# One root for the first two chunks, and a new order of all queues, in a gated recurrence with a convolution-gated output

## The chip, the cores and the metric

The kernel runs on one core of a Trainium2 chip. The metric is the device time of one execution in microseconds, given as the median of the runs. The engines are TensorE (PE), VectorE (DVE), ScalarE (ACT), GpSimd (POOL) and SyncE (SP), which issues nearly all DMAs.

## The reference

The inputs have 4 sequences of 6336 steps and 256 channels. With a = sigmoid(a_param), the first half is a gated linear recurrence:

```python
log_a = 8 * sigmoid(r_gate) * log(clip(a, 1e-6, 1 - 1e-6))
a_t   = exp(log_a)
xg    = sqrt(max(1 - a_t * a_t, 1e-6)) * sigmoid(i_gate) * x
h     = a_t[:, t] * h + xg[:, t]        # for each t; y[:, t] = h
```

The second half takes y: a causal convolution of 5 taps per channel gives a gate, and the result is `(sigmoid(conv(y)) * (y @ w_val)) @ w_out`, in float32.

## The kernel before

The 25344 rows (batch times steps) are cut into 51 windows w of 256 or 512 rows, and these into 28 chunks c (the table CHUNKS): chunks 0 and 1 are one window of 256 each (w0, w1), chunk 2 is one of 512 (w2), chunks 3 to 25 are two windows of 512 each (w3 and w4 to w47 and w48), chunk 26 is one of 512 (w49) and chunk 27 one of 256 (w50). Loads arrive with rows on the partitions; the recurrence needs channels on the partitions and time along the free axis, so PE transposes. Sigmoids are computed as tanh. A channel index has two halves h of 128.

There is no scheduler: the program is the string ORDER, read word by word, and each word emits one step. An engine executes its own steps in the order of the string, so ORDER fixes five queues, and waits follow from the data and from the buffers. A word is a step, its window or chunk, its half, and behind an @ the PSUM banks that it uses. The steps:

- `lr.w`, `li.w`, `lx.w` (L290, SP): load of a window of r_gate, i_gate or x. `st.w` (L519, SP): store of a window of the output. `s_wl.k`: loads of the weights; `s_wcast` (L273 to L276, POOL): their casts.
- `ta.c` (L308, ACT): tanh of r for a chunk. `tr.c.h` (L355, PE): its transposes, for a group of chunks (GROUPS). `ex.c.h` (L376, ACT): exp, which gives a_t for that group. `sq.c.h` (L384, POOL) or `sa.c.h` (L392, ACT): the square of it.
- `rt.b` (L403, ACT): the root of 1 - a_t*a_t for a batch of chunks (the table BATCHES). The root needs another table than exp and tanh, so ACT loads a table before and behind each visit (L535, `ACT_TABLE_LOAD`); several `rt` words with no tanh or exp between them are one visit.
- `tb.c` (L311, ACT): tanh of i. `pp.w` (L318, POOL): plus one. `up.w` (L330, POOL): times x. For w0 only `pp.0` and `up.0` are on POOL; for w1, w2 and w6, `xp.w` (L335, PE) copies x into PSUM by a product with the identity and `uv.w` (L344, DVE) does both.
- `nt.c` (L418, PE): the root, transposed back to rows. `xg.c` (L425, DVE): its product with the gated x. `xt.c` (L434, PE): that, transposed to channels.
- `sc.c.h` (L456, DVE): the recurrence as a scan along time.
- `cv.w` (L468, PE): the convolution as 20 matmuls with diagonal weights. `tg.w` (L475, ACT): its tanh. `vl.w` (L483, PE): y @ w_val. `gv.w` (L488, DVE): their product. `ou.w` (L498, PE): the product with w_out. `cd.w` (L506, DVE) or `ca.w` (L508, ACT): the copy of the result out of PSUM.
- `wm.k` (L362, PE): five matmuls of 512 columns with the identity whose result nobody reads.

An engine that stands at a step whose input is not there waits, and everything behind it on that queue waits too. For example, `rt` of the last chunks comes behind the `tg` words that precede it in ORDER, and `nt`, `xg`, `xt` and `sc` of these chunks behind `rt`. Loads are held back by their rings: r and i have four slots of a window each (`NRI`, `NII`), x has four (`NX`).

Of the kernel before, what the change touches and what calls it, by code (L numbers as in the profile page):

```python
# [44 lines left out]
tb.4 s_wcast xp.6@6,7 sc.3.0 tg.2 li.10 li.9 pp.5 ta.8 vl.1@4,5 lx.10 vl.2@2,3 uv.6 sq.6.1 vl.0@0,1 ta.7 gv.2 lr.17  # L45
cv.3@6,7 lx.8 sq.6.0 gv.0 ou.2.0@2,3 gv.1 tb.5 ou.0.0@0 cd.2.0 ou.1.0@1 up.5 tr.7.0@4,5 tg.3 cd.0.0 st.2 vl.3@2,3
lr.16 cd.1.0 ex.7.0 sq.5.1 st.1 tr.7.1@6,7 gv.3 lr.15 st.0 nt.4@0,1 li.12 ex.7.1 pp.7 cv.4@4,5 xg.4 sq.7.0
ou.3.0@2,3 tg.4 vl.4@6,7 cd.3.0 tb.6 pp.8 xt.4@4,5 gv.4 st.3 sq.7.1 li.11 lr.18 sc.4.1 ou.4.0@6,7 li.13 lx.9 wm.4@0
wm.12@0 up.8 rt.4 sc.4.0 pp.9 up.7 cd.4.0 cv.6@4,5 st.4 vl.6@6,7 lx.12 pp.10 li.14 nt.5@2,3 lx.11 sq.8.0 cv.5@0,1
tg.6 xg.5 tb.7 up.10 gv.6 xt.5@2,3 ou.6.0@6,7 sc.5.0 ta.9 li.16 up.9 vl.5@4,5 tg.5 lr.19 cd.6.0 ta.10 pp.11 wm.8@2  # L50
nt.6@0,1 gv.5 st.6 pp.12 li.15 xg.6 tb.8 ou.5.0@4,5 lr.22 up.11 tr.9.0@6,7 sc.5.1 ca.5.0 xt.6@0,1 ex.9.0 st.5
tr.9.1@4,5 lr.20 sc.6.0 lr.21 cv.7@2,3 ex.9.1 sq.8.1 up.12 cv.8@6,7 sc.6.1 tg.8 vl.7@4,5 pp.14 lx.16 lx.15 tg.7
nt.7@6,7 lx.14 sq.9.1 lx.13 tb.9 gv.7 cv.9@2,3 sq.10.1 xg.7 ou.7.0@4,5 tg.9 vl.9@0,1 cd.7.0 ta.11 sq.9.0 xt.7@2,3
gv.9 st.7 cv.10@4,5 li.20 ta.12 li.18 sc.7.0 pp.16 li.17 vl.8@0,1 sq.10.0 vl.10@6,7 tg.10 lr.26 li.19 gv.8
ou.9.0@4,5 pp.13 gv.10 wm.2@2 ou.8.0@0,1 rt.5 up.14 cd.9.0 ou.10.0@6,7 tr.11.1@2 sc.7.1 st.9 up.16 lr.25 cd.10.0
cv.11@4,5 up.13 cd.8.0 st.10 nt.8@6,7 lr.23 tr.11.0@3 st.8 pp.15 xg.8 tg.11 vl.11@0,1 lr.24 lx.18 ex.11.1 up.15
xt.8@6,7 gv.11 lx.17 ex.11.0 nt.9@4,5 sc.8.0 sq.11.1 tb.10 cv.12@0,1 tr.12.0@3 xg.9 ex.12.0 li.22 pp.17 li.21 sc.8.1
# [36 lines left out]
sc.24.0 tr.27.1@7 ca.40.0 cv.44@0,1 ex.27.1 up.47 st.40 cv.43@2,3 ex.26.1 lx.49 sc.24.1 tg.44 sa.27.1 nt.25@6,7
sq.26.1 tg.43 vl.42@0,1 sq.27.0 tb.26 xg.25 vl.44@2,3 sq.26.0 tb.27 vl.43@4,5 gv.42 pp.50 xt.25@6,7 pp.49 gv.44
# [9 lines left out]
def kernel(  # L105
# [82 lines left out]
    with tc.manual_schedule():  # L188
# [378 lines left out]
```

## Time and profile before

| | us |
|---|---|
| median of 3 runs (290.32 to 290.96) | 290.36 |
| the profiled execution, whole | 290.72 |
| its span, first to last instruction | 288.6 |
| ACT busy in it | 273.7 (95%) |
| PE busy | 250.6 (87%) |
| DVE busy | 247.0 (86%) |
| POOL busy | 241.5 (84%) |
| bytes moved | 104.76 MB, 363 GB/s over the span |

The whole time of the profiled execution is its span and 2.1 us around it. Busy times are read beside each other: idle time of an engine costs something only where another one waits for it. Rows of the timeline give start and duration in us from the span's start, the engine, the line and the step's form, and in brackets the idle time of that engine just before it with what ended it.

### The profile page before, as it was taken

The numbers are of one execution on the slowest core, as the hardware profiler recorded it, in microseconds if no ns is written. First come the engines' busy times: TensorE is split into PE (matmuls) and PEld (weight loads), VectorE is DVE, ScalarE is ACT, GpSimd is POOL, SyncE is SP. The second block draws the span as 40 slices with busy tenths as digits, with TensorE's granted clock in tenths as the row PEclk, the third lists the DMA queues.
The fourth block names the chain that finished last, engine by engine and source line by source line (L and its number), as shares of the span: only waits on it lengthen the run. The fifth ranks groups of instructions, "written<-read, shape, count | busy, mean of one in ns | idle before, by whom it ended". The sixth has DMA issues, their size and how long they took to land.

```text
span 288.6 us, 6363 instructions
## 1 busy us (share of the span) xinstructions
PE 250.6 (87%) x2552; PEld 169.4 (59%) x2552; DVE 247.0 (86%) x214; ACT 273.7 (95%) x197; POOL 241.5 (84%) x161
## 2 busy tenths in 40 slices
PE   2397799879898899889898999889799897999993
PEld 1253557547656677466567585467457664676552
DVE  5002899869999999999998999989999999999891
ACT  4999999999999999999999999999999999999754
POOL 1669469999999999999999999999998999496100
PEclk9999999999999999999999999999999999999998
DMA  7999999999999999999999999999999999885554
GB/s 240 396 392 409 407 374 385 357 385 371 403 407 410 410 395 366 375 346 417 418 408 341 376 413 414 418 395 396 351 352 412 420 386 408 263 292 208 199 221 182
DMA packets 29996, 104.76 MB, mean 363 GB/s; under 512 B 3335, under 2 KB 3854, under 8 KB 29966
## 3 DMA queue, kind: packets, MB, share of 16 engines
q1 hardware_dynamic: 29952, 104.35, 93.9%
q8 instruction: 20, 0.33, 0.5%
q14 instruction: 10, 0.08, 0.1%
q10 hardware_dynamic: 14, 0.01, 0.0%
HBM read 78.39 MB, written 25.95 MB: 362 GB/s over the span
## 4 chain that ended last, share of the span: by engine, by line
POOL 31%; PE 20%; DMA 15%; DVE 12%; ACT 12%; issue 7%; SPq 2%; DVEq 0%; ACTq 0%; POOLq 0%
POOL uring L330 14%; POOL ering L384 11%; DMA xring<-in_x_dram 8%; POOL tbring L318 6%; PE banks L468 6%; DMA iring<-in_i_gate_dram 6%; DVE yring L456 5%; DVE tgring L488 4%; PE banks L483 4%; PE banks L498 3%; PE banks L418 3%; ACT aring L376 3%; ACT tbring L311 3%; ACT ering L403 2%; SPq L290 2%
## 5 line engine op out<-in xcount | busy, mean ns | idle before, releaser
L330 POOL TENSOR_TENSOR uring<-tbring,xring 128x1024 bf16<-128x1024 bf16 (+1 forms) x48 | 100.9, 2116 | 11.1 <-DMA xring<-in_x_dram 10.6
L456 DVE TENSOR_TENSOR_SCAN yring<-aring,yring,banks 128x1024 bf16<-128x1024 f32 (+5 forms) x54 | 105.8, 1987 | 0.2
L384 POOL TENSOR_TENSOR ering<-aring 128x1024 f32<-128x1024 f32 (+2 forms) x54 | 91.7, 1715 | 14.7 <-ACT aring L376 14.6
L468 PE MATMUL banks<-yring,diag 64*64 64x512 bf16 (+7 forms) x1080 | 62.9, 361 | 4.6 <-DVE yring L456 3.6
L488 DVE SCALAR_TENSOR_TENSOR tgring<-tgring,banks 128x1024 bf16<-128x1024 bf16 (+1 forms) x51 | 59.3, 1178 | 5.1 <-PE banks L483 2.4
L498 PE MATMUL banks<-wo,tgring 128*128 128x256 bf16 x396 | 51.1, 274 | 7.5 <-DVE tgring L488 4.9
L376 ACT ACTIVATE aring<-banks,khf 128x2048 f32<-128x2048 bf16 (+3 forms) x38 | 53.9, 1467 | 0.4 <-PE banks L355 0.4
L475 ACT ACTIVATE tgring<-banks 128x1024 bf16<-128x1024 f32 (+1 forms) x51 | 50.5, 1007 | 3.0 <-PE banks L468 2.9
L318 POOL TENSOR_SCALAR tbring<-tbring 128x1024 bf16<-128x1024 bf16 (+1 forms) x48 | 49.0, 1030 | 4.4 <-ACT tbring L311 4.3
L498 PEld LDWEIGHTS <-tgring 128*128 128x128 bf16 x396 | 41.4, 114 | 18.6 <-DVE tgring L488 10.5
L483 PE MATMUL banks<-yring,wv 128*128 128x512 bf16 (+4 forms) x216 | 49.6, 361 | 1.6 <-ACT aring L376 0.8
L308 ACT ACTIVATE taring<-rring 128x2048 bf16<-128x2048 f32 (+2 forms) x28 | 47.6, 1718 | 2.4 <-DMA rring<-in_r_gate_dram 2.4
L311 ACT ACTIVATE tbring<-iring 128x2048 bf16<-128x2048 f32 (+2 forms) x28 | 47.9, 1719 | 0.0
L468 PEld LDWEIGHTS <-diag 64*64 64x64 bf16 x1080 | 29.1, 106 | 28.1 <-issue 11.6
L403 ACT ACTIVATE ering<-ering 128x4096 bf16<-128x4096 f32 (+5 forms) x15 | 44.7, 3016 | 0.1
L506 DVE COPY oring<-banks 128x1024 f32<-128x1024 f32 (+1 forms) x36 | 42.0, 1182 | 1.6 <-PE banks L498 1.1
L355 PE MATMUL banks<-ident_b,taring 128*128 128x128 bf16 x396 | 30.2, 230 | 9.4 <-ACT taring L308 7.2
L425 DVE TENSOR_TENSOR uring<-banks,uring 128x2048 bf16<-128x2048 bf16 (+2 forms) x28 | 30.4, 1093 | 6.7 <-PE banks L418 5.7
L355 PEld LDWEIGHTS <-taring 128*128 128x128 bf16 x396 | 26.1, 103 | 15.1 <-ACT taring L308 9.2
L483 PEld LDWEIGHTS <-wv 128*128 128x128 bf16 x216 | 19.9, 98 | 21.3 <-issue 7.1
L418 PE MATMUL banks<-ident,ering 128*128 128x128 f32 x198 | 29.7, 292 | 1.9 <-DVE yring L456 0.9
L418 PEld LDWEIGHTS banks<-ident,ering 128*128 128x128 f32 x198 | 25.9, 207 | 9.1 <-ACT ering L403 3.5
(45 smaller groups left out, 139.7 us busy)
## 6 DMA issues: line engine op xcount, KB each, us to landing
rring<-in_r_gate_dram SPq DMA_DIRECT2D x48, 512.0 KB, 7.9
iring<-in_i_gate_dram SPq DMA_DIRECT2D x48, 512.0 KB, 8.2
xring<-in_x_dram SPq DMA_DIRECT2D x48, 512.0 KB, 7.9
out_dram<-oring SPq DMA_DIRECT2D x48, 512.0 KB, 5.8
rring<-in_r_gate_dram SPq DMA_DIRECT2D x3, 256.0 KB, 4.4
iring<-in_i_gate_dram SPq DMA_DIRECT2D x3, 256.0 KB, 5.8
xring<-in_x_dram SPq DMA_DIRECT2D x3, 256.0 KB, 8.2
out_dram<-oring SPq DMA_DIRECT2D x3, 256.0 KB, 7.4
```

Of the source, the lines that this page charges most:

```text
L311: nc.scalar.activation(**tangent(c, tbring, NTI, iring, NII))
L318: nc.gpsimd.tensor_scalar(out=t, in0=t, scalar1=1.0, scalar2=1.0, op0=ALU.mult, op1=ALU.add)
L330: nc.gpsimd.tensor_tensor(out=u, in0=t1, in1=xt, op=ALU.mult)
L355: nc.tensor.transpose(out=bank[:, o:o + P], in_=taring[:, place(w, NTR), j, h * P:(h + 1) * P], identity=ident_b[:])
L376: nc.scalar.activation(out=dst, in_=src, func=ACT.Exp, scale=khf[:, h:h + 1], bias=khf[:, h:h + 1])
L384: nc.gpsimd.tensor_tensor(out=e, in0=a, in1=a, op=ALU.mult)
L418: nc.tensor.transpose(out=bank[:, k:k + P], in_=ering[:, e + q:e + wins[w] // 2:nq], identity=ident[:])
L456: nc.vector.tensor_tensor_scan(out=yring[:, h, col:col + o1 - o0], data0=aring[:, h, a_at[c] + o0:a_at[c] + o1], data1=xT[:, o0:o1], initi ...
L468: nc.tensor.matmul(out=gp[oh * 64:oh * 64 + 64, h, a:b], lhsT=diag[half * 64:half * 64 + 64, h, k, :], rhs=yring[half * 64:half * 64 + 64, ...
L483: nc.tensor.matmul(out=val[:, m, a:b], lhsT=wv[:, hk, m * P:(m + 1) * P], rhs=yring[:, hk, col:col + b - a], start=(hk == 0), stop=(hk == ...
L488: nc.vector.scalar_tensor_tensor(out=tgring[:, w % NTG, :, 0:wins[w]], in0=tgring[:, w % NTG, :, 0:wins[w]], scalar=1.0, in1=live.pop(("va ...
L498: nc.tensor.matmul(out=ops[:, j * D:(j + 1) * D], lhsT=gv[:, hk, j:wins[w]:J], rhs=wo[:, hk, :], start=(hk == 0), stop=(hk == H - 1))
```

## The change

Three things change, all in tables; no function does.

- BATCHES: chunks 0 and 1 form one batch, so the first two roots become one instruction, and there are 11 batches in place of 12 (a later `rt.b` has a number lower by one).
- ORDER: all five queues are in a new order, and the PSUM banks behind the @ are new. Among it: SP loads lr.0, lr.1 and li.0 first; the first root visit takes chunk 2, then 0 and 1, then 3 and 4; `xp.1`, `uv.1`, `gv.1` and `cd.1` come earlier; `s_wcast` comes ahead of `sq.5.0`; `cv.45` and `tg.45` come ahead of the last root in place of behind it; `lx.50` is issued ahead of st.44 and st.43.
- Five groups `wm` stand in place of eleven. The copies of windows 5, 23, 34 and 39 move from ACT to DVE, those of 17, 33 and 38 from DVE to ACT.

```diff
-BATCHES = [[0], [1], [2], [3, 4], [5, 6, 7], [8, 9, 10], [11, 12, 13], [14, 15, 16], [17, 18, 19], [20, 21, 22],
-    [23, 24, 25], [26, 27]]
+BATCHES = [[0, 1], [2], [3, 4], [5, 6, 7], [8, 9, 10], [11, 12, 13], [14, 15, 16], [17, 18, 19], [20, 21, 22], [23,
+    24, 25], [26, 27]]
...
-s_ident s_small s_kt s_diag lr.2 lr.0 s_wl.3 lr.1 li.0 lr.3 s_wl.2 ta.2 ta.0 lr.4 tr.0.1@0 ta.1 lr.6 tr.2.0@1 tb.0
-lr.5 tr.1.0@2 tr.0.0@3 tr.2.1@4 ex.2.0 li.1 tr.1.1@5 li.2 ex.1.1 li.3 ex.0.1 sq.1.1 lx.0 ex.1.0 li.4 sq.2.0 ex.0.0
-ex.2.1 sq.1.0 ta.3 sq.2.1 pp.0 sq.0.0 ta.4 sq.0.1 tb.1 lr.10 tr.3.0@4,5 tb.2 lr.9 lr.8 tr.3.1@2,3 lr.7 ex.3.0 lx.2
-s_wl.1 up.0 lx.1 ex.3.1 sq.3.0 lx.4 lx.3 wm.10@6 tb.3 sq.3.1 ta.6 pp.4 wm.5@6 wm.3@6 wm.9@6 wm.6@6 sq.4.1 lr.13 ta.5
-li.5 li.6 sq.4.0 li.7 xp.2@2,3 lr.14 pp.3 rt.0 tr.5.0@4,5 lx.6 uv.2 rt.2 up.4 nt.0@0 rt.1 xg.0 rt.3 xt.0@0,1 xp.1@2
-sc.0.0 up.3 nt.1@3 lx.5 nt.2@0 uv.1 s_wl.0 xg.1 xg.2 xt.1@2,3 lx.7 sc.0.1 lr.12 nt.3@0,1 sc.1.0 lr.11 xt.2@6,7
-sc.1.1 ex.5.0 xg.3 tr.5.1@2,3 li.8 sc.2.0 xt.3@0,1 ex.5.1 sq.5.0 cv.0@4,5 sc.2.1 tg.0 sc.3.1 cv.1@6,7 cv.2@2,3 tg.1
+s_ident s_small s_kt s_diag lr.0 lr.1 li.0 s_wl.2 s_wl.3 lr.2 lr.3 ta.0 lr.4 tb.0 ta.1 lr.5 tr.0.1@0 tr.1.1@1
+tr.1.0@2 ta.2 ex.0.1 ex.1.0 lr.6 li.1 tr.2.0@3 tr.0.0@0 tr.2.1@4 ex.2.0 ex.0.0 ex.2.1 li.2 lx.0 li.4 li.3 sq.1.0
+sq.2.0 sq.0.1 sq.0.0 pp.0 ex.1.1 ta.3 wm.17@5 ta.4 wm.13@5 tb.1 tr.3.1@0,1 tb.2 lr.10 up.0 ex.3.1 lr.9 lr.8 lr.7
+lx.1 tr.3.0@4,5 lx.2 li.5 ex.3.0 sq.4.1 lx.3 lx.4 tb.3 ta.6 li.7 ta.5 xp.1@4 sq.2.1 sq.4.0 lr.11 s_wl.1 xp.2@0,1
+uv.1 sq.3.0 sq.1.1 sq.3.1 s_wl.0 rt.1 rt.0 pp.3 pp.4 rt.2 nt.2@4 lr.14 lx.6 li.6 nt.0@5 uv.2 nt.1@3 lr.12 lr.13 xg.0
+xg.1 li.8 tr.5.0@6,7 lx.5 xt.0@0,1 sc.0.1 up.3 sc.0.0 tr.5.1@2,3 up.4 xt.1@0,1 xg.2 ex.5.0 sc.1.0 sc.1.1 nt.3@4,5
+s_wcast xt.2@0,1 lx.7 cv.1@6,7 ex.5.1 xg.3 sc.2.0 sq.5.0 vl.1@4,5 tg.1 gv.1 cv.0@2,3 tb.4 vl.0@6,7 ou.1.0@0 sq.6.1
+xp.6@4,5 cd.1.0 ta.8 sc.2.1 st.1 xt.3@0,1 li.9 li.10 pp.5 uv.6 lx.8 tg.0 sq.6.0 ta.7 gv.0 cv.2@2,3 nt.4@6,7 up.5
...
-ou.42.0@0,1 rt.11 gv.43 ou.44.0@2,3 up.49 ca.42.0 sc.25.1 ou.43.0@4,5 ca.44.0 st.42 cv.45@0,1 ca.43.0 st.44
-cv.46@2,3 sc.25.0 st.43 lx.50 nt.26@7 tg.46 vl.46@4,5 xg.26 tg.45 cv.47@2,3 gv.46 vl.47@0,1 tg.47 ou.46.0@4,5 gv.47
-up.50 vl.45@2,3 ca.46.0 nt.27@0 ou.47.0@6,7 gv.45 st.46 xt.26@4,5 ca.47.0 xg.27 ou.45.0@2,3 sc.26.0 st.47 cv.48@6,7
+tg.44 lx.49 vl.44@6,7 tb.26 sq.27.0 sq.26.0 sq.26.1 xg.25 cv.45@4,5 vl.43@0,1 gv.44 vl.45@2,3 sa.27.1 tb.27 tg.45
+pp.49 gv.43 xt.25@4,5 gv.45 sc.25.1 sc.25.0 rt.10 ou.44.0@0,1 ou.43.0@6,7 ca.44.0 ou.45.0@2,3 ca.43.0 st.44
+cv.46@0,1 nt.26@6 pp.50 up.49 nt.27@7 ca.45.0 st.43 st.45 vl.46@2,3 up.50 cv.47@4,5 tg.46 xg.26 xg.27 gv.46
+xt.26@0,1 tg.47 vl.47@6,7 cv.48@2,3 gv.47 tg.48 ou.46.0@4,5 sc.26.1 vl.48@6,7 ca.46.0 sc.26.0 ou.47.0@2,3 xt.27@4,5
```

More of the change, by code (lines that the diff above doesn't have):

```diff
@@ L48 @@
[L48 to L57, printed above, removed]
@@ new lines @@
+gv.6 xt.5@2,3 sc.5.0 cv.5@4,5 ta.10 li.15 li.16 ou.6.0@6,7 wm.15@0 nt.6@0,1 tg.5 cd.6.0 ta.9 vl.5@6,7 sc.5.1 st.6
+up.10 pp.12 lr.22 lr.21 lr.20 tr.9.1@4,5 gv.5 tb.8 xg.6 tr.9.0@2,3 ex.9.1 lr.19 ou.5.0@6,7 xt.6@0,1 cd.5.0 ex.9.0
+cv.8@4,5 sc.6.1 st.5 up.12 pp.11 pp.14 pp.13 up.11 cv.7@6,7 tg.8 lx.14 li.18 li.17 lx.13 vl.8@2,3 nt.7@4,5 tg.7
+sc.6.0 vl.7@6,7 tb.9 ta.12 xg.7 cv.10@0,1 lr.25 gv.7 xt.7@4,5 ta.11 gv.8 ou.7.0@6,7 cv.9@2,3 cd.7.0 tg.10 sc.7.0
+st.7 sq.10.1 sq.9.0 sq.10.0 sq.9.1 lx.16 tr.11.1@6 tg.9 ou.8.0@0,1 lx.15 cd.8.0 pp.16 tr.12.1@7 vl.9@2,3 rt.4 gv.9
@@ new lines @@
+st.8 vl.10@0,1 lr.24 lr.26 sc.7.1 ou.9.0@2,3 up.14 up.13 cd.9.0 cv.11@4,5 up.16 pp.15 st.9 gv.10 nt.8@2,3 li.19
+lr.23 ou.10.0@0,1 xg.8 ex.12.1 ex.11.1 tg.11 cd.10.0 xt.8@2,3 tr.11.0@7 st.10 sc.8.0 lx.17 tr.12.0@6 vl.11@0,1 tb.10
+sq.11.1 li.20 li.21 ex.12.0 up.15 gv.11 lx.18 li.22 nt.9@4,5 cv.12@0,1 ex.11.0 ou.11.0@6,7 sc.8.1 ta.14 xg.9 pp.18
+pp.17 cv.14@2,3 tg.12 cd.11.0 xt.9@4,5 sq.11.0 up.17 sq.12.0 st.11 ta.13 cv.13@0,1 sc.9.0 lx.20 lr.30 lr.29 tg.14
+tr.13.0@6,7 tg.13 lx.21 nt.10@2,3 sc.9.1 ex.13.0 vl.13@0,1 up.18 gv.13 tb.11 tr.13.1@4,5 vl.12@6,7 lx.22 xg.10
@@ new lines @@
+pp.23 sq.14.0 pp.24 up.24 sc.11.0 li.28 ex.15.1 lr.34 lr.33 lr.32 gv.18 cv.20@6,7 tb.14 up.23 sq.15.1 sc.12.0
+tr.15.0@4,5 tg.20 ex.15.0 ou.18.0@2,3 cv.19@6,7 cd.18.0 sc.12.1 st.18 vl.19@2,3 tg.19 sq.15.0 sq.16.0 lx.26 lr.31
+li.29 lx.25 vl.20@4,5 tb.15 nt.13@6,7 cv.21@0,1 gv.20 ta.18 ou.20.0@4,5 tg.21 sq.16.1 gv.19 xg.13 vl.21@2,3
+ou.19.0@6,7 cd.20.0 xt.13@0,1 st.20 gv.21 pp.25 pp.26 lx.27 cd.19.0 up.26 up.25 cv.22@4,5 vl.22@2,3 ou.21.0@6,7
+st.19 li.30 sc.13.0 cd.21.0 wm.19@0 pp.27 rt.6 sc.13.1 st.21 nt.14@6,7 lx.28 tg.22 up.27 xg.14 cv.23@0,1 ta.17 gv.22
@@ new lines @@
+xt.14@6,7 pp.28 tg.23 tr.17.1@4,5 sc.14.0 lr.37 lr.38 lr.36 lr.35 vl.23@2,3 ex.17.1 lx.29 lx.30 ou.22.0@0,1 gv.23
+cv.24@4,5 tb.16 sq.18.1 cd.22.0 tr.17.0@2,3 sc.14.1 tg.24 li.33 li.34 up.28 ou.23.0@0,1 nt.15@4,5 ex.17.0 pp.30
+vl.24@6,7 xg.15 ta.20 cv.25@2,3 pp.29 sq.17.0 xt.15@4,5 cd.23.0 gv.24 st.23 li.31 cv.26@0,1 st.22 sc.15.0 li.32
+up.29 ta.19 tg.25 ou.24.0@6,7 tg.26 tr.19.0@2,3 cd.24.0 ex.19.0 up.30 vl.25@0,1 sq.18.0 nt.16@6,7 st.24 sc.15.1
+lr.42 lx.32 lr.40 tr.19.1@2,3 tb.18 lx.31 xg.16 cv.27@4,5 ex.19.1 gv.25 xt.16@6,7 sc.16.1 sq.19.0 sq.17.1 tg.27
@@ new lines @@
+tb.17 sq.19.1 ou.25.0@0,1 vl.27@2,3 cv.28@4,5 cd.25.0 tg.28 gv.27 st.25 pp.31 sq.20.1 pp.32 vl.28@0,1 lr.39 lx.33
+vl.26@4,5 gv.28 lx.34 ou.28.0@0,1 ou.27.0@2,3 lr.41 li.36 sc.16.0 li.35 up.32 up.31 pp.33 cd.28.0 rt.7 gv.26
+cv.29@6,7 cv.30@0,1 cd.27.0 tg.30 ou.26.0@4,5 nt.17@2,3 cd.26.0 st.26 xg.17 vl.29@4,5 tg.29 li.37 lx.35 ta.21 gv.29
+li.38 xt.17@2,3 lx.36 pp.34 up.34 up.33 sc.17.0 ta.22 vl.30@6,7 tr.21.1@4 tr.21.0@5 nt.18@0,1 tb.19 li.40 gv.30
+sq.20.0 xg.18 tr.22.0@2 ex.21.1 ex.22.0 li.39 sc.17.1 xt.18@0,1 ex.21.0 ou.29.0@6,7 pp.35 lr.43 tr.22.1@2 lr.44
@@ new lines @@
+lr.45 lr.46 st.27 cd.29.0 tb.20 cv.31@3,4 pp.36 up.35 sc.18.1 lx.38 cv.32@6,7 tg.31 up.36 st.28 ex.22.1 sc.18.0
+lx.37 tg.32 vl.32@4,5 nt.19@2,3 tb.21 ou.30.0@6,7 vl.31@0,1 sq.21.1 sq.21.0 st.29 gv.32 xg.19 gv.31 lx.39 ta.23
+cv.33@4,5 sq.22.1 xt.19@2,3 tg.33 cd.30.0 ta.24 sc.19.0 st.30 ou.31.0@0,1 cv.34@4,5 lx.40 lr.48 vl.34@6,7 tg.34
+pp.39 pp.37 gv.34 sq.22.0 lr.47 pp.38 vl.33@4,5 up.38 li.41 rt.8 cd.31.0 sc.19.1 tr.23.1@6,7 li.42 up.37 gv.33 pp.40
+ou.32.0@0,1 cv.35@2,3 cd.32.0 ou.34.0@4,5 nt.20@0,1 up.39 cd.34.0 tg.35 xg.20 st.34 lx.42 ex.23.1 vl.35@4,5 st.31
@@ new lines @@
+lr.49 sc.22.0 ou.38.0@4,5 li.47 lx.46 vl.39@2,3 lx.45 li.48 cv.40@6,7 gv.39 up.43 sc.22.1 nt.23@2,3 vl.40@0,1 xg.23
+tg.40 tb.24 ou.39.0@6,7 gv.40 xt.23@2,3 ca.38.0 cv.42@0,1 st.38 cd.39.0 st.39 pp.46 pp.45 ou.40.0@4,5 tg.42 lx.47
+cv.41@6,7 sc.23.1 up.46 ca.40.0 ta.26 st.40 vl.42@0,1 lx.48 sc.23.0 tg.41 li.50 nt.24@4,5 up.45 li.49 tb.25
+tr.26.1@3 gv.42 cv.43@6,7 xg.24 vl.41@0,1 gv.41 pp.48 tr.26.0@2 xt.24@4,5 pp.47 ex.26.1 tg.43 ex.26.0 ou.42.0@6,7
+sc.24.1 up.47 ou.41.0@2,3 ca.42.0 cv.44@0,1 ca.41.0 st.42 sc.24.0 tr.27.1@5 st.41 lx.50 nt.25@2,3 up.48 ex.27.1
@@ L101 @@
+vl.50@6,7 tg.50 ca.49.0 gv.50 st.48 st.49 ou.50.0@6 ca.50.0 st.50
 """
```

58 lines of the change are left out of this document (15 added, 43 removed).

## The prediction

> **What bounds the kernel now.** I read the engine table and the slices of the page first (busy us, share of the span, instructions; then the busy tenths of each fortieth of the span), because the change touches every queue and the question is which of them has room.
>
> ```profile
> PE 250.6 (87%) x2552; PEld 169.4 (59%) x2552; DVE 247.0 (86%) x214; ACT 273.7 (95%) x197; POOL 241.5 (84%) x161
> ...
> PE   2397799879898899889898999889799897999993
> ...
> DVE  5002899869999999999998999989999999999891
> ACT  4999999999999999999999999999999999999754
> POOL 1669469999999999999999999999998999496100
> ```
>
> ScalarE (ACT) is full from the second slice on until the last three; VectorE (DVE) starts late and is then nearly as full. So the total is a start, a full middle, and a tail. The windows by stage (busy us per engine, granted clock, DMA share) say what each of these has left.
>
> ```profile
> 36.00:72.00 36.00, 32.65 (x326) 21.89 (x325) 31.39 (x27) 35.73 (x24) 33.60 (x24) 1.00 0.99 375
> 72.00:108.00 36.00, 33.20 (x377) 22.88 (x374) 34.63 (x27) 35.57 (x24) 35.84 (x22) 1.00 1.02 406
> 252.00:270.00 18.00, 17.93 (x194) 12.08 (x190) 18.00 (x12) 17.85 (x21) 12.62 (x10) 1.00 0.76 276
> 270.00:289.00 19.00, 14.15 (x148) 8.91 (x140) 10.70 (x12) 9.38 (x11) 1.17 (x1) 0.92 0.43 170
> ```
>
> From 36 to 72 DVE still has 4.6 us of idle time, from 72 to 108 1.4 us. From 252 to 270 PE, DVE and ACT are all full. Third, the timeline of ACT, PE and DVE at the start, at DVE's two longest later waits, and at the end (start, duration, what, in brackets the idle time before it and its releaser):
>
> ```profile
> 6.67 0.63 ACT L308 ACTIVATE taring<-rring 128x512 bf16<-128x512 f32 x1 [0.86 <-DMA rring<-in_r_gate_dram]
> ...
> 27.35 5.61 ACT L403 ACTIVATE ering<-ering 128x512 bf16<-128x512 f32 x4
> ...
> 262.69 1.49 ACT L403 ACTIVATE ering<-ering 128x1536 bf16<-128x1536 f32 x1
> 264.09 2.82 ACT L508 COPY oring<-banks 128x1024 f32<-128x1024 f32 x3
> 266.93 1.28 ACT L535 ACT_TABLE_LOAD   x1
> ```
>
> ```profile
> 14.90 2.74 PE L355 MATMUL banks<-ident_b,taring 128*128 128x128 bf16 x24 [0.77 <-ACT taring L308]
> 17.44 6.77 PE L362 MATMUL banks<-ident_b 128*128 128x512 bf16 x25
> 25.47 1.96 PE L335 MATMUL banks<-xring,ident 128*128 128x512 f32 x4 [1.27 <-DMA xring<-in_x_dram]
> 27.27 1.06 PE L355 MATMUL banks<-ident_b,taring 128*128 128x128 bf16 x16
> 284.39 0.61 PE L498 MATMUL banks<-wo,tgring 128*128 128x256 bf16 x4 [0.85 <-DVE tgring L488]
> ```
>
> ```profile
> 28.66 0.42 DVE L425 TENSOR_TENSOR uring<-banks,uring 128x512 bf16<-128x512 bf16 x1 [0.45 <-PE banks L418]
> 63.47 1.22 DVE L425 TENSOR_TENSOR uring<-banks,uring 128x2048 bf16<-128x2048 bf16 x1 [2.24 <-PE banks L418]
> 188.89 2.35 DVE L425 TENSOR_TENSOR uring<-banks,uring 128x2048 bf16<-128x2048 bf16 x2 [1.48 <-PE banks L418]
> ```
>
> ACT runs without a break from 6.67, and the last root ends at 264.18. DVE first gets work from a root at 28.66, and waits for a root's transposes at 63.47 and 188.89. The last matmul of the kernel starts at 284.39.
>
> **The change, by sums.** ACT: two 128x512 roots (0.62 each) become one of 1024 (1.04): 0.2 us less. The first visit to the root table took four root instructions before and three after, and both orders have nine visits, so the 18 table loads (1.28 each) stay. One ACT copy of an output (1.01) becomes a DVE copy (1.21). PE loses six groups of unread matmuls; the late groups took 1.08 each, so 6.5 us, three of them after 36 us. PE waits for others anyway until 240 and has no gap over 0.25 us from 240 to 283.5, where no group stood, so their direct gain is nothing. POOL and the bytes moved are unchanged. So the sums give ACT -1.2 and DVE +1.2: nothing that could decide. The rest is position.
>
> **The start.** The new SP order loads the two 256-column windows and li.0 before lr.2. The bytes up to lr.2 are 1.44 MB, against 1.11 MB landed by 6.65 before; at the 348 to 390 GB/s of those slices lr.2 lands at about 7.5 and ta.2 ends at 8.5, where the exponentials started at 7.85 before. ACT runs 0.65 late, and since nothing idles behind it, this stays. The r loads behind ta.3 and ta.4 on SP, and with them lx.1 and lx.2, move by about as much; li.5 between the two x loads is behind lx.2 and harmless.
>
> The first root visit then starts at 28.1 with rt.1 (chunk 2), then the merged rt.0, which ends at 30.1; before, chunk 0 had its root at 27.98. sq.1.1, which the merged root needs, stands behind sq.4.1, sq.2.1, sq.4.0 and sq.3.0 on POOL (they wait for ex.3, then 1.04 to 1.9 each): done at 26.1, so 3 us of cover. On PE nt.2 is ahead of nt.0; with 0.95 and 0.25 for them xg.0 starts at about 30.7 to 31.6, some 2 to 3 us later. But a second wait eats most of it: gv.1 is now ahead of sc.2.1 and sc.3 on DVE, and tg.1 ends only at 39.5 behind ex.5.0 and ex.5.1, so DVE would wait there up to 2 us. From there (gv.1, ou.1, cd.1, sc.2.1 to 42.9, then the queue at 0.58 to 2.33 per instruction) DVE reaches the common set gv.4, sc.4 at 62.4 instead of 60.1: 2.3 late. At xg.5 both DVE queues have exactly the same work ahead, and there the old order idled 2.24 us. So at xg.5 I carry 0.5 us. POOL gains: the casts of s_wcast stand where it idled (4.27 us before sq.5.0; the casts themselves then waited 1.99 for their load), so it is some 2 us ahead.
>
> **The middle.** Behind xg.5 DVE has one copy more ahead of gv.44 (+1.1 with the 0.1 us by which instructions overlap). Its waits over 0.25 us from there to 252 sum to 4.0 us; the one of 1.48 at xg.17 goes, because the root of chunks 17 to 19 has 2.9 us less ACT work ahead. I count that one and leave the other 2.5 for the range. gv.44: 262.33 + 1.1 + 0.5 - 1.5 = 262.4, as before.
>
> **The tail.** Ahead of the last root ACT has tg.45 more and 0.2 us of root less (+0.8): with the 0.65 from the start it ends at 265.6. Behind it stand three copies (2.8), the table load (1.28), tg.46 and tg.47: DVE ends gv.47 at 274.1 and then needs sc.26 (2 x 1.15), gv.48, sc.27, gv.49 and gv.50, PE from ou.44 on has cv.45 and vl.45 (1.20 + 0.87) less than before, 19.4 us instead of 21.5. Walked through, gv.50 ends at 282.1, ca.50 at 283.3 (285.6 before), and with the same 3.0 us for the last store the span is 286.3; PE's work alone gives 288.6 - 2.07 = 286.5. lx.50, which came late before (POOL waited 6.79 us for it at 273.16), is now issued ahead of st.44 and st.43. Three convolutions stand closer to their tanh: tg.31, tg.43 and tg.45 have 1.6 to 2.6 us too little if DVE saves no more than I counted, nothing if it saves all 4.0. These shifts lie on one queue and do not add up beyond the largest. Between 0 and 2.6 I take 0.9, nearer to nothing, because the 2.5 us of DVE waits that I did not count stand ahead of them. Span 287.2, that is 1.4 less. Against the profiled execution (290.72, 2.1 around its span) that is 289.3; the median was 0.36 below it, so 289.0.
>
> **The pace of TensorE.** The granted clock reads 1.00 in every window up to 270, yet the rows show two paces: 24 transposes in 2.74 us at 14.90 (114 ns each), 16 in 1.06 at 27.27 (66). The 25 unread matmuls lie between: the first five took 2.13 us, the last five 1.08. So some 5 us of unbroken work brought the fast pace, and the old order kept PE at work up to 24.21, 1.27 us before the first x product. In the new order ten unread matmuls stand ahead of tr.3, and PE would be idle from about 17.5 until lx.1 lands near 25. At the slow pace xp.1 and xp.2 take 5.6 instead of 2.8 us and nt.2, nt.0 some 0.9 more; the wait at gv.1 covers nearly all of that, but tr.5.0 would come about 0.5 us late for ex.5.0, which nothing covers, and tr.5.1 again. I price it at 0 to 1.0 us.
>
> The Trainium skill (TensorE: Matmul & The Clock Gate, Part 1) says that TensorE starts at half rate, reaches full rate after about 3.4 us of sustained work and falls back after an idle window of that length. By that rule the 7 us pause makes the first x products slow, and the end of my price that holds is the upper one. The trace agrees on the way up; no run here shows the way down.
>
> **The rivals.** (1) ScalarE starts to wait for convolutions: slower. If DVE is not back at xg.5 but stays 2.3 late, tg.45 and with it the last root come 2.6 + 2.0 = 4.6 us late, and 286.3 + 4.6 = 290.9, so 292.7. It decides from about 3.2 us of such waits. For it: ACT had under 0.5 us idle per 36 us from 72 on, so each wait is lost. Against it: the 2.24 at 63.47 and 4.0 us later are there to be filled. (2) Order changes little, since the work of the full engines is the same to 1.2 us: waits of 1.5 to 3 us, or the slow pace in the start and 1 us of waits, give spans of 288 to 289.3, 289.8 to 291. (3) DVE saves all 4.0: PE is then ready early, but the last root at 265.6 still sets the tail: 286.3 less at most 0.5, so 287.6.
>
> **How the numbers follow.** 0.3% (0.9 us) is about what a measurement of this kernel can tell from no change. Forecast and (3) together 0.48, both faster; (2) 0.19, within; (1) 0.33, slower. The range from 287.4 to 292.8 reaches from (3) to the price of (1).
>
> **What would show it.** Right: xg.0 near 31, DVE's wait before gv.1 near 39, xg.5 within 1 us of 63.5, the last root's end near 265.6 to 267, and ca.50 below 285. Wrong: ACT waits for PE at L475 of over 3 us in sum before the last root, or transposes at 114 ns after 30 us.

## The result, and the profile after

The changed kernel takes 292.86 us (median of four, 292.34 to 293.54) against 290.34: 1.0091 of the time before, with an interval of 1.0073 to 1.0108. It is slower by 2.5 us, where 1.4 us less was forecast. The profiled execution took 292.75, of which 289.8 are the span. Its span is only 1.2 us longer than that of before; this execution is the mildest of the four (the others have spans of 290.6 to 291.6 and a mean granted clock of 0.977 or 0.978, where it has 0.986), so about half of the loss is on no trace.

The page's engine table and slices, as shown of before:

```profile
PE 243.0 (84%) x2496; PEld 164.5 (57%) x2522; DVE 248.3 (86%) x215; ACT 272.7 (94%) x195; POOL 241.7 (83%) x161
...
PE   2525879959997899798999999877979997999993
...
ACT  4899999999999999989999999999999999999854
...
PEclk9995999999999999999999999999999999999999
```

The sums came out nearly as worked out (ACT -1.0, DVE +1.3). New is the 5 in the row of the granted clock: the fourth fortieth, 21.7 to 29 us. The windows by stage:

```profile
36.00:72.00 36.00, 30.31 (x315) 20.46 (x318) 32.32 (x27) 35.94 (x24) 33.60 (x21) 1.00 0.99 386
72.00:108.00 36.00, 32.78 (x381) 23.48 (x382) 35.42 (x28) 35.91 (x25) 33.82 (x21) 1.00 1.01 395
108.00:144.00 36.00, 32.28 (x326) 21.17 (x330) 34.92 (x26) 35.09 (x23) 35.77 (x22) 1.00 1.00 388
252.00:270.00 18.00, 17.89 (x183) 12.31 (x181) 17.30 (x13) 17.02 (x19) 16.73 (x13) 1.00 0.74 271
```

The columns behind the length are PE, PEld, DVE, ACT and POOL, busy us with instructions. ACT is as full as before up to 108, but idles 0.9 us between 108 and 144, and 1.0 between 252 and 270, where it was full before. The timeline of ACT, at the start, at one of the new waits and at the last root:

```profile
8.37 1.06 ACT L308 ACTIVATE taring<-rring 128x1024 bf16<-128x1024 f32 x1 [2.10 <-DMA rring<-in_r_gate_dram]
...
28.25 2.00 ACT L403 ACTIVATE ering<-ering 128x1024 bf16<-128x1024 f32 x2
...
128.50 1.91 ACT L311 ACTIVATE tbring<-iring 128x2048 bf16<-128x2048 f32 x1 [0.86 <-DMA iring<-in_i_gate_dram]
...
267.05 1.49 ACT L403 ACTIVATE ering<-ering 128x1536 bf16<-128x1536 f32 x1
```

And PE and DVE at the places that the prediction spoke of:

```profile
25.17 4.91 PE L335 MATMUL banks<-xring,ident 128*128 128x512 f32 x6 [7.42 <-ACT taring L308]
...
39.59 0.69 DVE L488 SCALAR_TENSOR_TENSOR tgring<-tgring,banks 128x512 bf16<-128x512 bf16 x1 [1.72 <-ACT tgring L475]
...
63.74 1.21 DVE L425 TENSOR_TENSOR uring<-banks,uring 128x2048 bf16<-128x2048 bf16 x1
...
188.87 1.22 DVE L425 TENSOR_TENSOR uring<-banks,uring 128x2048 bf16<-128x2048 bf16 x1
...
245.18 1.23 PE L418 MATMUL banks<-ident,ering 128*128 128x128 f32 x8 [1.30 <-ACT ering L403]
```

Most of the walk is there: the pause of PE to 25.17 and slow x products behind it, the wait at gv.1 near 39, no wait left at 63.7 or 188.9. But the last root ends at 268.54 (264.18 before, 265.6 forecast), and PE now waits 1.30 for a root at 245, where before had no wait for a root (it had one of 0.90 for DVE at 243.82). ca.50 ends at 286.84 (before 285.63).

How ACT's time between the root of chunks 5 to 7 and the last root changed is one window in each trace, from end to end of these roots (before, then after; length, busy us, instructions):

```profile
62.04:264.18 202.14, 200.73 (x139) 1.00 0.99 380
```

```profile
62.41:268.54 206.13, 202.32 (x140) 1.00 0.98 378
```

4.0 us more: 1.6 of busy time and 2.4 of waiting (1.41 became 3.81). Of the 1.6, 0.4 is longer rows in sum, and 1.1 is that neighbouring rows overlap less (11.2 us in place of 12.3).

### The profile page after: what moved, and what is told of

It is laid out like the page before. It is cut to its first block, busy times and chain, and to the rows that moved or that the text cites. A ratio compares the mean times of both kernels' runs of the same rounds, so it can differ in the third digit from the quotient of the medians.

```text
span 289.8 us, 6268 instructions
## 1 busy us (share of the span) xinstructions
PE 243.0 (84%) x2496; PEld 164.5 (57%) x2522; DVE 248.3 (86%) x215; ACT 272.7 (94%) x195; POOL 241.7 (83%) x161
## 4 chain that ended last, share of the span: by engine, by line
PE 28%; DMA 21%; ACT 16%; DVE 13%; issue 9%; POOL 7%; SPq 4%; DVEq 0%; ACTq 0%; POOLq 0%
PE banks L468 9%; DMA rring<-in_r_gate_dram 9%; DMA iring<-in_i_gate_dram 8%; PE banks L498 7%; ACT aring L376 5%; DVE yring L456 5%; PE banks L483 4%; DMA out_dram<-oring 4%; ACT taring L308 4%; POOL uring L330 4%; PE banks L434 3%; DVE oring L506 3%; SPq L290 3%; ACT tbring L311 3%; PE banks L418 3%
## 5 line engine op out<-in xcount | busy, mean ns | idle before, releaser
L468 PE MATMUL banks<-yring,diag 64*64 64x512 bf16 (+7 forms) x1080 | 64.3, 362 | 7.7 <-DVE yring L456 3.8
L475 ACT ACTIVATE tgring<-banks 128x1024 bf16<-128x1024 f32 (+1 forms) x51 | 50.3, 1003 | 3.0 <-PE banks L468 3.0
L483 PE MATMUL banks<-yring,wv 128*128 128x512 bf16 (+7 forms) x190 | 48.2, 359 | 4.3 <-ACT tgring L475 1.3
L311 ACT ACTIVATE tbring<-iring 128x2048 bf16<-128x2048 f32 (+2 forms) x28 | 48.1, 1721 | 2.1 <-DMA iring<-in_i_gate_dram 2.1
L506 DVE COPY oring<-banks 128x1024 f32<-128x1024 f32 (+1 forms) x37 | 43.8, 1187 | 3.0 <-PE banks L498 1.4
L403 ACT ACTIVATE ering<-ering 128x4096 bf16<-128x4096 f32 (+4 forms) x14 | 44.6, 3218 | 0.1
L355 PE MATMUL banks<-ident_b,taring 128*128 128x128 bf16 x396 | 28.3, 223 | 8.5 <-ACT taring L308 7.7
L355 PEld LDWEIGHTS <-taring 128*128 128x128 bf16 x396 | 24.4, 99 | 14.6 <-ACT taring L308 10.9
L434 PE MATMUL banks<-ident,uring 128*128 128x128 f32 x198 | 27.2, 278 | 5.2 <-DVE uring L425 4.5
L418 PE MATMUL banks<-ident,ering 128*128 128x128 f32 x198 | 29.0, 289 | 2.5 <-ACT ering L403 1.7
```

What stands on the lines that cost most here:

```text
L311: nc.scalar.activation(**tangent(c, tbring, NTI, iring, NII))
L355: nc.tensor.transpose(out=bank[:, o:o + P], in_=taring[:, place(w, NTR), j, h * P:(h + 1) * P], identity=ident_b[:])
L468: nc.tensor.matmul(out=gp[oh * 64:oh * 64 + 64, h, a:b], lhsT=diag[half * 64:half * 64 + 64, h, k, :], rhs=yring[half * 64:half * 64 + 64, ...
L483: nc.tensor.matmul(out=val[:, m, a:b], lhsT=wv[:, hk, m * P:(m + 1) * P], rhs=yring[:, hk, col:col + b - a], start=(hk == 0), stop=(hk == ...
L506: nc.vector.tensor_copy(out=dst, in_=src)
```

## The experiments

Two theories stood against each other. **Start:** ACT gets its first inputs late and PE is slow behind its pause, and this delay is carried to the end. **Order:** the late order loses by itself, because ACT waits for convolutions and PE for roots.

### Undoing the cold start

**e1_warm.** After, with six unread groups behind tr.3.0, so that PE stays at work up to the x products.

```diff
 tr.3.0@4,5
+wm.20@6 wm.21@6 wm.22@6 wm.23@6 wm.24@6 wm.25@6
```

> The changed kernel with six more groups of unread matmuls (bank 6) behind tr.3.0, where TensorE was idle from 17.8 to 25.2 us; six groups at the 1.08 us of the fast pace take 6.5 us of that. Theory A, the slow pace of TensorE at the first x products costs the start and the later stages feel it: granted clock above 0.99, xp.1 and xp.2 in 2.8 us in place of 4.9, and 1.0 to 2.0 us less, 290.9 to 291.9. Theory B, the order behind the start is what costs: the pace returns, but DVE and ACT wait at gv.1 anyway, and the time stays within 0.5 us of the changed kernel, 292.4 to 293.4.

292.12 us, 1.0065 [1.0040, 1.0090] of before. By the medians 0.7 of the 2.5 came back; the interval overlaps that of after, so even this is not told from nothing. The six x products took 3.17 in place of 4.91, but the clock then fell to 0.85 and 0.72 in the two windows from 36 to 44 us. The last root is still 4.0 late. The slow x products are not the main cause.

**e2_cold.** Before, without its five groups of the start.

```diff
-wm.10@6 wm.5@6 wm.3@6 wm.9@6 wm.6@6
```

> The kernel before without its five groups of unread matmuls at the start (17.4 to 24.2 us), so TensorE is idle there; nothing else is changed. Theory A (the pace costs): the first x products take 3.9 in place of 1.96 us and 1.0 to 2.0 us more in all, 291.4 to 292.4. Theory B (the order costs): within 0.5 us of 290.3.

292.50, 1.0064 [1.0040, 1.0089]. The old order pays 1.8 us by the ratio for the same pause, and from 63 us on every milestone of its trace (xg, root, gv) is late by 1.8 to 2.0: the old order passes a delay of the start on undiminished. Two rows are longer behind the pause: the four x products, 3.75 in place of 1.96, and the 16 transposes that took 1.06 at 27.27 in before and for which ACT now waits 1.50 at 37.58.

```profile
28.55 1.91 PE L354 MATMUL banks<-ident_b,taring 128*128 128x128 bf16 x16
```

(This kernel's lines are one lower.) In the changed order the six x products stand together ahead of these transposes, and the pace is back at them: 1.06.

### Old start, new start

**e3_old_start, e4_new_start.** The orders cut at st.4, near 61 us, and joined crosswise.

```diff
(the edit in words)
-ORDER = one order
+ORDER = before up to st.4, then what is left of the changed order      (e3)
+ORDER = the changed order up to st.4, then what is left of before      (e4)
```

> The order of before up to and with st.4 (about 61 us; then both VectorE queues have the same work behind them), and everything left in the changed order. Two single roots for chunks 0 and 1, and the old five groups at the start. Theory A (the start costs): near the kernel before or under it, 289.5 to 291.0. Theory B (the order behind 61 us costs): near the changed kernel, 292.0 to 293.2.

> The changed order up to and with st.4, with the merged root, and everything left in the order of before. Theory A: near the changed kernel, 291.8 to 293.0. Theory B: near the kernel before, 289.9 to 290.9.

e3: 292.72, 1.0071 [1.0046, 1.0096]; e4: 291.54, 1.0049 [1.0028, 1.0070]. In e4 the trace is 1.5 late at xg.5 and 2.0 at the end: the new start up to 61 us costs 1.4 by itself, by the ratio. But e3, without it, lost as much. Its trace has waits of 1.91 and 0.77 before tb.8 and tb.9 (L311, for li loads) at 71 us that neither parent has: the joint itself cost up to 2.7, so e3 does not tell what the late order is worth.

**e7_merged_only.** Before with `BATCHES` starting `[[0, 1], [2], ...]` and the merged root in the place of the first.

```diff
-BATCHES = [[0], [1], [2], [3, 4], ...
+BATCHES = [[0, 1], [2], [3, 4], ...
```

> The kernel before with the merged root of chunks 0 and 1 alone, at the place of the first root; the order is otherwise unchanged. ScalarE has 0.2 us less ahead of the root of chunks 3 and 4, chunk 0 has its root 0.4 us later. Theory C (a delay of the first scans passes on undiminished): 290.2 to 290.7. Rival, ScalarE sets the pace from the first visit on: 289.8 to 290.1.

290.31 against 290.22: 1.0006 [0.9984, 1.0028]. The merged root by itself is not told from nothing.

### Joints that cost too much

**e5_new_to_223, e6_old_to_223, e9_new_tail, e10_old_to_135, e11_new_to_135.** Four more cuts: at gv.35 (223 us), at xg.25 (260) and at up.23 (135).

```diff
(the edits in words)
+ORDER = the changed order up to gv.35, then what is left of before     (e5)
+ORDER = before up to gv.35, then what is left of the changed order     (e6)
+ORDER = before up to xg.25, then what is left of the changed order     (e9)
+ORDER = before up to up.23, then what is left of the changed order     (e10)
+ORDER = the changed order up to up.23, then what is left of before     (e11)
```

> The changed order up to and with gv.35 (about 223 us), then everything left in the order of before. Theory C, three prices that add: a later start passes to the end undiminished, ScalarE waits more in the changed middle (about 1 us from 61 to 223), and TensorE loses about 2 us between 234 and 247 in the changed tail, which is full from there to the end: without the changed tail 291.0 to 292.0. Theory D, the tail costs nothing and is even the shorter one, by the 2.07 us of cv.45 and vl.45 that it has done earlier: 292.6 to 294.

> The order of before up to and with gv.35 (about 223 us), with the single roots, then everything left in the changed order. Theory C: the changed tail alone costs 1.0 to 2.0 us, 291.2 to 292.2. Theory D: it gains, 288.2 to 290.0.

> The order of before up to xg.25 (260 us), the changed order behind it: cv.45 and tg.45 ahead of the last root. Merged root and new start not in it. In after, ca.50 ended 18.3 us behind the last root (286.84 - 268.54), in before 21.45. Theory A (the new tail is worth what I predicted, and what was lost is that ScalarE came late to the last root): ScalarE is as early as in before, the root ends at 264.2 + 2.0 for tg.45 and ca.42 ahead of it = 266.2, ca.50 at 284.5, 1.1 less: 289.1. Rival B (the tail is bound by PE or DVE, the late root cost nothing): ca.50 within 0.4 of 285.6, time within 0.3% of before. Rival C (tg.45 waits for its convolution and takes the root with it): ca.50 over 286.2, slower.

> The order of before up to up.23 (135 us), with the merged roots as in before, the changed order behind it; at this place the two orders differ by 7 steps only. Theory A (in after the first part costs 1.4 us, the second is worth nothing or a loss of its own, since ScalarE waits for convolutions and PE for roots from 170 on): 0.5 to 2 us slower than before, 290.8 to 292.3, and the last root's end 3 to 4 us later than in before. Rival B (all of the loss is in the start): ca.50 at 283.5, 288.4.

> The changed order with its merged root up to up.23 (135 us), before's order behind it. Theory A: the delay of the start comes through as in the kernel with only the new start (1.0049): 1.2 to 2.2 us slower, 291.4 to 292.4, rigid from 140 on. Rival B (all of the loss is in the start): 2.5 slower, 292.7. Rival C (the waits of before's order in the middle take the delay up): within 0.9 of before.

e5 297.61 (1.0253 [1.0230, 1.0276]), e6 295.53 (1.0175 [1.0151, 1.0199]), e9 295.76 (1.0186 [1.0162, 1.0210]), e10 293.31 (1.0103 [1.0074, 1.0132]). e5, e6 and e9 are slower than both parents, and e10 is not told from after, the slower of the two: at 223 the trace of e6 falls from 0.8 ahead of before at 215 us to 7.0 behind at 237, in e9 DVE waits 4.19 and 2.78 behind the joint, in e10 1.81. They tell nothing of the late order or the tail. e11 is readable: 292.41, 1.0092 [1.0059, 1.0126]. Its trace is 0.5 late at xg.5, 1.57 at tb.13, ahead of the joint, and 1.7 from 150 to the end. Before's order passes on what the changed order has lost up to 135.

### The unread groups behind 36 us

**e8_no_late_unread.** Before without them, to try "their direct gain is nothing".

```diff
-wm.4@0 wm.12@0 wm.8@2 wm.2@2 wm.16@6 wm.18@2
```

> The kernel before without its six groups of unread matmuls behind 36 us (the five at the start stay). Theory C has no price for them, since they stand where TensorE waits anyway: 289.9 to 290.5, fast pace throughout. Rival, they keep the pace: the granted clock falls below 0.99 and the time rises by 0.5 to 2 us.

292.85, 1.0092 [1.0066, 1.0117]: they are worth 2.6 us in before. Where wm.4 and wm.12 stood, PE now pauses 3.42 us, and the next rows show what that starts (the first two are windows by stage, the third is the timeline of PE):

```profile
60.00:64.00 4.00, 2.33 (x21) 0.93 (x21) 2.73 (x2) 3.98 (x3) 4.00 (x4) 0.50 1.00 393
64.00:68.00 4.00, 4.00 (x31) 2.50 (x32) 0.67 (x1) 3.99 (x4) 4.00 (x3) 0.66 1.02 377
```

```profile
61.67 2.35 PE L468 MATMUL banks<-yring,diag 64*64 64x512 bf16 x20 [3.42 <-DVE yring L456]
```

The convolution takes 2.35 in place of 1.27, and xg.5 loses 2.4 us more against before than cd.4 ahead of it on DVE. (cd.4 was 1.5 late already, because ACT's first exp came at 9.86, in before at 7.83; the edit does not reach that far back.) After, with three late groups, reads 1.00 from 32 us on in its trace. e12 and e17 below have the same groups there and do not, so it is open whether its order needs fewer.

### Undoing the order of the first loads

**e12_old_loads_warm.** The changed order, but before's words up to ex.3.1 (18 us), which load lr.2 first; six unread groups; li.25, which was taken for the load that tb.13 waited for, issued ahead of lx.24 and st.15.

```diff
-s_ident s_small s_kt s_diag lr.0 lr.1 li.0 s_wl.2 s_wl.3 lr.2 lr.3 ta.0 lr.4 tb.0 ta.1 ...
+s_ident s_small s_kt s_diag lr.2 lr.0 s_wl.3 lr.1 li.0 lr.3 s_wl.2 ta.2 ta.0 lr.4 tr.0.1@0 ta.1 ...
+wm.20@6 wm.21@6 wm.22@6 wm.23@6 wm.24@6 wm.25@6
...
-lr.27 lx.24 gv.15 cv.17@0,1 gv.16 ou.15.0@4,5 ... st.15 li.25
+lr.27 li.25 lx.24 gv.15 cv.17@0,1 gv.16 ou.15.0@4,5 ... st.15
```

> The changed order behind ex.3.1 (18 us), with before's order up to there (lr.2 first), six groups of unread matmuls behind tr.3.1, and li.25 issued ahead of lx.24 and st.15. Theory A (the start's loads 1.4 us, the slow pace 0.7, the wait for li.25 0.9): ScalarE has no wait over 0.5 us at 127, root 25 within 1 us of before, last root 1 to 2 us earlier than in after, 290.3 to 291.3. Rival B (the late order loses by itself however early it starts): last root still 3 us or more behind before's, 292.

290.04, 1.0001 [0.9982, 1.0020]: the whole loss is gone, with the late order in place. But li.25 was the wrong load. Chunk 13 is windows 23 and 24, so tb.13 needs li.24; in after that was issued at 120.19 and landed at 128.34, and li.25, issued at 126.02, landed at 133.33, when tb.13 was done (timeline of SP in after):

```profile
120.19 0.84 SPq L290 DMA_DIRECT2D iring<-in_i_gate_dram  x1
...
126.02 0.42 SPq L290 DMA_DIRECT2D iring<-in_i_gate_dram  x1
```

The trace (of an execution of 291.71) shows a fall of the pace at 64 us, behind two pauses of 1.31 and 2.04 us within 7 us (window, then timeline):

```profile
64.00:68.00 4.00, 3.25 (x28) 1.77 (x28) 4.00 (x4) 4.00 (x3) 4.00 (x4) 0.67 1.01 396
```

```profile
66.12 2.35 PE L468 MATMUL banks<-yring,diag 64*64 64x512 bf16 x20
```

**e13_mended, e14_late_i, e15_new_loads, e16_cold.** e13 is e12 with a group in each of these two pauses. e14, e15 and e16 are e13 with one mended place put back: li.25, the first loads, the cold start.

```diff
+wm.26@6
 ou.3.0
...
+wm.27@0
 xt.5
```

> The kernel with before's loads up to ex.3.1, six unread groups in the start and li.25 early (290.04), and two more unread groups in the pauses of 1.31 and 2.04 us that PE has at 57.6 and 62.7 in it (ahead of ou.3, and ahead of xt.5). In the profile of that kernel the granted clock fell to 0.67 at 64 to 68 and cv.5 took 2.35 us in place of 1.27. Theory A (that fall is what set its slower runs, span 289.5 to 290.2, apart from those of 287.7 to 288.6): no window between 32 and 280 under 0.97, all spans under 288.7, median 289.4 to 290.0. Rival B (the fall is covered by DVE's waits): as before the two groups, 290.0, with the same spread.

> The mended kernel with li.25 where the changed order has it (behind st.15). Theory A: tb.13 waits 0.9 us at 127 and the last root comes by as much later: 0.5 to 0.9 us over the mended one. Rival B (the wait is taken up by later ones): equal within 0.3.

> The changed order with its own loads at the start (lr.0, lr.1, li.0 ahead of lr.2), but with the six unread groups of the start, li.25 early and the two groups at 57 and 63: the mended kernel but for the loads. Theory A: ta.2 waits 2 us and ScalarE is 1.0 to 1.5 us late from then on; part of it comes through: 0.7 to 1.4 us over the mended one, 290.3 to 291.2. Rival B (DVE's wait at gv.1 and xg.5 covers it, as I predicted for delays of the start): within 0.3 of the mended one.

> The mended kernel without the six unread groups of the start, so that PE idles from about 18 to 25 us. Theory A: the clock falls to 0.50 at 20 to 28, 0.5 to 1.0 us over the mended one. Rival B (with ScalarE early, the slow pace is covered): within 0.3. Rival C (as in before without its five groups): 1.8 us over it.

e13: 289.80, 0.9981 [0.9963, 0.9999], no window of 4 us between 4 and 284 under 0.97, and spans from 287.3 to 289.1. e14: 290.51, 1.0001 [0.9977, 1.0025]; e16: 290.46, 1.0006 [0.9985, 1.0027]: their intervals overlap that of e13, so li.25's place and the cold start are not told from nothing here. For li.25 that fits, since tb.13 does not use it. e15: 291.34, 1.0035 [1.0015, 1.0056], 1.5 us over e13. But its trace does not show this as a late start: its first exp came at 8.44, in e13 at 8.73, and its pace fell to 0.81 and 0.76 at 36 to 44 us. So it does not price the loads, and the next pair tries them by themselves.

**e17_old_loads_only, e18_new_loads_only.** One part each: the change with before's words up to ex.3.1 and nothing else, and before with the changed words up to ta.4 and nothing else. Each is a block of some 18 us on all queues: besides the loads it moves ta and ex on ACT, tr on PE and squares on POOL, and e17 loses the unread groups wm.17 and wm.13.

```diff
-... lr.0 lr.1 li.0 s_wl.2 s_wl.3 lr.2 ...
+... lr.2 lr.0 s_wl.3 lr.1 li.0 lr.3 s_wl.2 ...       (e17; the other way round in e18)
```

> The changed order with one part undone: before's order of the loads and steps up to ex.3.1 (18 us, lr.2 first). No unread groups added, li.25 where the change put it. Theory A (the new loads cost 1.5 us and that comes through to the end): 291.0 to 291.6, against 292.86 with the change's own loads. Rival B (the loads matter only together with a warm TensorE): 292.4 or more.

> Before with one part of the change: the changed order up to ta.4 (lr.0, lr.1, li.0 ahead of lr.2; without its two unread groups), before's order behind it, all of before's unread groups in place. Theory A (lr.2 lands later, ta.2 waits 1.4 to 2.1 us, and before's order passes a delay on): 1.2 to 1.6 us slower, 291.4 to 291.8, rigid from 63 to the end. Rival B (what the new loads cost comes from the pauses of PE behind them): within 0.5 of before.

e17: 289.83, 0.9979 [0.9962, 0.9996]: with before's first 18 us the change is 0.45 us **faster** than before, 3.0 us better than as it was made. e18: 291.75, 1.0040 [1.0024, 1.0055]: the changed first 18 us make before slower by 1.5 (medians) or 1.2 (ratio). Three rows of ACT in e17, and one of PE, to be held against after's:

```profile
4.38 1.57 ACT L308 ACTIVATE taring<-rring 128x1024 bf16<-128x1024 f32 x2 [1.36 <-DMA rring<-in_r_gate_dram]
...
128.10 1.90 ACT L311 ACTIVATE tbring<-iring 128x2048 bf16<-128x2048 f32 x1
...
266.16 1.49 ACT L403 ACTIVATE ering<-ering 128x1536 bf16<-128x1536 f32 x1
```

```profile
25.86 5.13 PE L335 MATMUL banks<-xring,ident 128*128 128x512 f32 x6 [7.93 <-DMA xring<-in_x_dram]
```

ta.2 starts at 4.38 and the first exp at 7.67 (after: 8.37 and 9.33). The cold start is still there, with six x products in 5.13. tb.13 does not wait for li.24, although ACT came to it at 127.64 in after and 0.46 later here; so a late ACT is not what brought that wait. Of the other traces only e5 has it (0.64).

How the two traces part: after is 1.5 us behind e17 at ta.3 (12.45 for 10.94) and still 1.0 at the end of the root of chunks 5 to 7 (62.41 for 61.38). Then the pace of PE falls in e17, behind pauses of 1.30 and 2.16 us, and a convolution takes 2.35 (window by stage):

```profile
64.00:68.00 4.00, 3.84 (x29) 1.97 (x30) 3.55 (x4) 3.31 (x2) 4.00 (x4) 0.58 1.01 406
```

That costs e17 1.6 us, and from 78 to 126 after is the earlier one on ACT, by 0.56. The waits for loads of i at tb.13 and tb.20 turn it round, and ca.50 ends 0.8 later in after. So this pair of traces (executions of 292.75 and 290.84) shows 0.8 of the 3.0 us at the end, or 2.4 without the fall in e17, which is an estimate.

In e18 a late load shows again, with a wait of 2.59:

```profile
9.24 1.06 ACT L308 ACTIVATE taring<-rring 128x1024 bf16<-128x1024 f32 x1 [2.59 <-DMA rring<-in_r_gate_dram]
```

## Why the prediction was wrong

**The step that failed is the first term: lr.2 landed by about 7.5, and ACT 0.65 us late.** In the trace of after lr.2 landed at 8.35, and the first exp came at 9.33 for 7.83 in before, 1.5 late. Undoing the first 18 us is worth 3.0 us (after against e17). The working took the loads as landing one after the other. The chain of waits in after and the row of what the DMAs moved (slices of 0.25 us from 0 to 10, first after, then before) show what happened:

```profile
3.40 4.95 DMA rring<-in_r_gate_dram
```

```profile
GB/s 0 0 0 0 0 0 4 197 229 311 365 295 401 393 303 377 357 152 131 86 66 57 180 315 352 340 455 361 410 344 393 426 393 393 442 344 475 377 393 442
...
GB/s 0 0 0 0 0 0 35 231 0 147 279 410 360 442 287 389 401 328 369 221 238 295 344 418 352 385 279 385 426 344 434 352 438 332 279 426 442 328 393 410
```

Summed slice by slice, 1.43 MB had landed at 7.0 in after, for 1.65 in before; the dip at 4.25 to 5.75 is deeper in after. But lr.2 was complete only at 8.35, when 1.96 MB had: the loads issued behind it had taken a share of half a MB. That was to be read in before already. The 1.11 MB of the working are the bytes issued up to lr.1; at 6.65, when lr.1 was there, 1.52 MB had landed. In before lr.2 was the first load of all, issued at 0.72; in the new order it is issued at 3.40, behind five others, with two more of its size right behind it (4.02 and 4.57). The landing differs from trace to trace, so one pair of traces is weak evidence. The first exp came at 8.44 to 10.20 in the seven traces with the new loads (lr.2 landed at 7.45 to 9.21), and at 7.34 to 9.86 in the thirteen with the old ones. The middle values, 9.18 and 7.83, are 1.35 apart, twice the 0.65.

"Since nothing idles behind it, this stays" was right for before's order: e18 is 1.5 to 2.0 late at every milestone from xg.5 to the end. In the new order it did not stay: against e17 the 1.5 became 1.0 by 62 us, and against before 0.4, because the new order gains on the way (e17 is 0.66 ahead of before there). Why the first 18 us then cost 3.0 in the change, and 1.2 to 1.5 in before, is open: the traces show a part of it. That the loads are what counts in the block is read from ACT's waits for them; no run moves the loads alone.

**The rest of the start held in its numbers, and in part by luck.** First root visit at 28.25 (28.1 forecast), xg.0 at 30.88 (30.7 to 31.6), tg.1 read by gv.1 at 39.59 after 1.72 of waiting (39.5, up to 2), xg.5 at 63.74 (63.5 to 64). The 28.1 was worked out from a first exp at 8.5; with 9.33 the way from there to the root was 0.7 shorter than thought, and the two errors nearly met.

**The slow pace** was bounded by 0 and 1.0. e1 gives 0.7 back and e16 loses 0.7 to e13, neither clear of noise. By the Trainium skill (TensorE: Matmul & The Clock Gate, Part 1), PE falls back to half rate after an idle window of about 3.4 us. The way down, which no run had shown, agrees for the pauses of 7.42 (0.50 at 24 to 28) and 3.42 us (e8). The rule does not tell the cases of e12 and e17, where no pause there was over 2.16 us and the pace fell; after has 1.31 and 1.97 at the same place, and its pace did not. The measurement decides, and a pause of 2 us is not safe in this kernel. That the upper end of the price would hold does not follow: in e17 the pause is there and the time is 289.83.

**"Their direct gain is nothing"** was argued from PE's gaps, and it was the wrong question: the late groups hold the pace, 2.6 us in before (e8). (Before's trace also has two gaps over 0.25 us in the stretch from 240, 0.51 at 240.44 and 0.90 at 243.82.) In after's trace it did no harm, since the pace holds from 32 us on with three of them.

**The middle** held at the wait of 1.48 before xg.17, which is gone (188.87). The last root did not: 268.54 for 265.6. Of the 4.36 over before, 0.4 was there at 62 us, 1.6 is busy time where I had 0.8, and 2.4 is new waiting of ACT, where the allowance was 0.9 in all. This allowance is the second term that was too small. Of the 2.4, 1.1 are waits for loads of i (tb.13 0.86, tb.20 0.23), 0.5 more for transposes ahead of exp, and 0.6 the copy ca.42; the waits for convolutions (L475) are 0.6 in both traces. In e13 2.88 of idle time are left between the same roots, 1.5 over before: much the same waits without those for i, and again 0.6 at L475. So of the **Order** theory a part holds, but not the reason that it gives for ACT: the late order leaves ACT more idle time ahead of the last root, and not more of it for convolutions. That this is why e17 and e13 gain 0.4 rather than 1.4 is likely and not shown.

**The tail** held: 18.30 from the last root's end to that of ca.50 (17.7 forecast, 21.45 before). It pays back 3.15 of the root's 4.36.

**The rivals.** Rival (1) had the size, 292.7, and the last root over 4 us late, but by luck: neither its condition, DVE 2.3 late at xg.5, nor its waits for convolutions came. The two signs of being wrong did not come either (0.6 at L475 in place of over 3; 16 transposes in 1.06), while two of the signs of being right failed, the last root and ca.50. After's profiled execution has 2.95 around its span, against 1.7 to 2.1 in the other three and 2.1 in before, so 0.8 of the 2.0 by which it is longer than before's lie outside the span; why is open.

## What to carry to other kernels

The first inputs of the engine that is full to the end can decide the time of the whole kernel: do not count a load as landed when the bytes up to it have, since in these traces what was issued behind it had a share of the transfer. A rebuilt order is best judged by undoing its first 20 us alone before its middle is blamed. Joining two orders in the middle measured mostly the joint; putting one start on each of the two orders measured the start, as a block. Find out from the table of chunks which load a step waits for before moving one. And one trace is one execution: the first exp came up to 1.8 us apart in the traces with the new loads, and 2.5 in those with the old.

## What the runs showed of the hardware

- The granted clock can read 1.00 while PE runs at the slow pace: in e17 the windows from 16 to 36 all read 1.00, with the x products at 5.13 for six (its trace has no record of the clock before about 31 us; that of after begins at about 13); in after they read 0.82, 0.50 and 0.83 with 4.91. Durations of like rows (transposes of 114 and 66 ns) tell the pace, the column does not always.
- Five unread matmuls in a pause of PE can be worth over a microsecond somewhere else: 20 matmuls of a convolution took 2.35 us instead of 1.27 behind a pause of 3.42 (e8), and in two traces behind one of 2.04 and 2.16 (e12, e17); behind one of 1.97 in after they took 1.28.
- A load is complete later than the bytes up to it: 1.44 MB were issued up to lr.2, and 1.96 MB had landed when it was complete (1.7 to 2.2 in the seven traces with the new loads).
